# Attention beside a long convolution: QK tiles of 32 rows, zero-weight matmuls in idle row groups, and fillers placed by array use

## The chip, the cores and the metric

The kernel runs on one NeuronCore of one Trainium2 chip. The metric is the device time of one execution in microseconds. The profile is one execution recorded by the hardware profiler; its span is somewhat longer than the timed runs.

## The reference

Two branches work on the same input of 2,048 positions and 448 features and are blended by a gate.

```
q = (x @ wq) in 16 heads of 28;  k = x @ wk;  v = x @ wv     # one k and v for all heads
p = softmax(q k^T / sqrt(28));   a = concat_heads(p v) @ wo
K[d,l] = Re sum_n C[d,n] * exp(dt[d]*A[d,n]*l) * dt[d]*B[d,n]   # N = 256, l = 0..2047
b = causal_convolution(u, K) + u * Dskip                        # written with FFTs of length 4096
out = g * a + (1 - g) * b;       g = sigmoid(sum(x * gate_w))
```

## The kernel before

**Attention.** The scores are made transposed: keys on the 128 output partitions, 512 queries along the free dimension. There are 1,024 such tiles (16 groups of four heads and 512 queries, times 16 key blocks, times 4 heads). A tile is one QK matmul (L1126) whose contraction has 29 rows: 28 features and one row that carries a bound subtracted from the scores. Head h of a group lies on partitions 32h onwards, so that the four heads use the four row groups of the array, each as a tile of 32 rows by 128 columns. `main` packs the tiles into 410 sets, of three heads and two heads in turn; a set fills three or two banks of psS, which has six, so that one set can be made while ScalarE turns the other into exponentials (L1142, one instruction a set). When four tiles of one key block are there, a PV set (L1151) runs: four matmuls of 128 rows by 32 columns, side by side in the column groups, adding into the bank psB. After 16 key blocks psB holds a finished group, ScalarE copies it out, and it is normalised and projected (L1022).

**Convolution.** VectorE builds tables of complex powers (`masters`, `tables`), TensorE turns them into kernel values (`kgen`, L938: 128x32 tiles, 64 columns streamed), these pass through DRAM and come back as Toeplitz tiles T, and `conv` (L985: 128x32 tiles, 128 columns streamed) applies them; L1005 (128x64 tiles) transposes the result, and VectorE adds it to the output.

**Order.** `Prog.op` records each operation with a planned duration `ns`, a mode (`q`: 32x128, `c`: 128x32, `h`: 128x64, `f`: 128x128) and, on TensorE, a number `st` for what it contributes to array activity. `schedule` is a list scheduler that lays all engines out in advance; a change of mode costs 105 ns in the plan (`SWITCH`). Each engine then runs its list strictly in order, with semaphores between engines.

**Fillers.** After scheduling, `fill` walks TensorE's order. Where the plan leaves a gap, it looks at up to eight windows of 3,413 ns, sums `st` in them, and if the sum is under `SCORE` it inserts n filler matmuls with zero weights (each unit planned as `FILL` ns and worth `UNIT`). They write zeros into psB while a PV accumulation is open there (`opened`, start=False), or into an unused bank early on. A filler takes the mode of its neighbours: `q` (L626: one matmul of 32 rows by 128 columns), `f` (L629: one of 128x128) or `c` (L633: four of 128x32). A unit streams 128 columns in all three.

Of the kernel before, what the change touches and what calls it, by code (L numbers as in the profile page):

```python
# [11 lines left out]
P = 128  # L12
# [4 lines left out]
DH = 28  # L17
# [16 lines left out]
RING = 15  # L34
# [45 lines left out]
class Prog:  # L80
# [17 lines left out]
    def op(self, eng, fn, ns, rd=(), wr=(), pr=0, lat=None, lock=None, unlock=None, comm=None, mode="f", st=None, slk=None):  # L98
        o = Op()
        o.i, o.eng, o.fn, o.ns, o.lat, o.pr = len(self.ops), eng, fn, ns, 0, pr  # L100
        o.lock, o.unlock, o.slot, o.ndma = lock, unlock, None, 0
        o.comm = comm
        o.mode, o.slk = mode, slk
        o.st = st or (0.0075 * ns if eng == "pe" else 0.0)
        o.lat = self.LAT[eng] if lat is None else lat
        deps = {}
        if comm is not None:
            for k in comm:
                deps[self.lastw[k]] = 1
                self.commops.setdefault(k, []).append(o.i)  # L110
        for k in rd:
            for c in self.commops.get(k, ()):
                deps[c] = 1
            w = self.lastw.get(k)
            if w is not None:
                deps[w] = 1
        for k in wr:
            w = self.lastw.get(k)
            if w is not None:
                deps[w] = 1  # L120
            for r in self.readers.get(k, ()):
                deps.setdefault(r, 0)
        for k in rd:
            self.readers.setdefault(k, []).append(o.i)
        for k in wr:
            self.lastw[k] = o.i
            self.readers[k] = []
        deps.pop(o.i, None)
        o.deps = deps
        self.ops.append(o)  # L130
        return o
# [222 lines left out]


class Kernel:
    FILL = 90.0
    WIN = 3413.0
    UNIT = 0.56
    SCORE = 17.0  # L360
    nfill = 0

    def __init__(self, nc, ins, out):
# [250 lines left out]
    def fill(self):  # L614
        pg = self.pg
        order, out = pg.order["pe"], []
        used = min(i for i, x in enumerate(order) if pg.ops[x].lock is not None and pg.ops[x].lock.bank == 5)
        opened, prev = False, None

        def filler(n, mode, bank, acc):  # L620
            t, bo = self.bank(bank)

            def fn(e):
                for _ in range(n):
                    if mode == "q":
                        r = e.matmul(t.v(0, P, bo, [[1, 128]]), self.zero.v(0, 32, 0, [[1, P]]), self.ident.v(0, 32, 0, [[1, P]]),  # L626
                                     start=not acc, stop=False, tile_position=(0, 0), skip_group_check=True)
                    elif mode == "f":
                        r = e.matmul(t.v(0, P, bo, [[1, 128]]), self.zero.v(0, P, 0, [[1, P]]), self.ident.v(0, P, 0, [[1, P]]),  # L629
                                     start=not acc, stop=False, tile_position=(0, 0), skip_group_check=True)  # L630
                    else:
                        for j in range(4):
                            r = e.matmul(t.v(32 * j, 32, bo, [[1, 128]]), self.zero.v(0, P, 0, [[1, 32]]), self.ident.v(0, P, 0, [[1, P]]),  # L633
                                         start=not acc, stop=False, tile_position=(0, 32 * j), skip_group_check=True)
                return r
            o = Op()
            o.i, o.eng, o.fn, o.ns, o.lat, o.pr, o.mode = len(pg.ops), "pe", fn, 0, 0, 0, mode
            o.lock = o.unlock = o.slot = o.comm = None
            o.ndma, o.extra, o.end = 0, 0, 0.0
            o.deps = {self.zop.i: 1, self.iop.i: 1}  # L640
            pg.ops.append(o)
            return o.i
        act = [(o.end - o.lat - o.ns, o.st) for o in (pg.ops[x] for x in order)]
        for k, x in enumerate(order):
            o = pg.ops[x]
            start = o.end - o.lat - o.ns
            if prev is None:
                e0, m0 = max(self.zop.end, self.iop.end) + 60.0, "f"
            else:
                e0, m0 = prev.end - prev.lat, prev.mode  # L650
            room = start - e0 - (pg.SWITCH if m0 != o.mode else 0.0) - 60.0
            need = 0.0
            if room > self.FILL and (opened or k < used):
                for w0 in range(8):
                    a = e0 - self.WIN * w0 / 8.0
                    got = sum(d for u, d in act if a <= u < a + self.WIN)
                    need = max(need, self.SCORE - got)
            n = int(min(room, need * self.FILL / self.UNIT) / self.FILL)
            if n > 0:
                mode = m0 if m0 in ("c", "f") else o.mode if o.mode in ("c", "f", "q") else "q"  # L660
                out.append(filler(n, mode, 6 if opened else 5, opened))
                act.append((e0, self.UNIT * n))
                self.nfill += n
            out.append(x)
            pv = self.pvs.get(x)
            if pv is not None:
                opened = pv < 15
            prev = o
        pg.order["pe"], self.wact = out, act
# [250 lines left out]
    def kgen(self, c, sub=None):  # L920
        pg = self.pg
# [5 lines left out]
        whole = sub is None  # L927
# [3 lines left out]
        for jj in range(8):  # L931
            def mm(e, comp, jj=jj):
                for half in range(2):
                    for g in gs:
                        o = 64 * (g // 2) + 16 * half + 8 * (g % 2) + jj
                        fo = lo + comp * BLK + EW + o
                        mo = FM + comp * 64 + o - 32 * (g // 2)
                        r = e.matmul(  # L938
                            G.v(32 * g, 32, 64 * jj, [[1, 64]]),
                            tab.v(0, P, lo + comp * BLK + 32 + o, [[EW, 32]]),  # L940
                            tab.v(0, P, fo, [[mo - fo, 2], [EW, 32]]),
                            start=(comp == 0 and half == 0), stop=(comp == 1 and half == 1),
                            tile_position=(0, 32 * g), skip_group_check=True)
                return r
            for comp in range(2):
                pg.op("pe", lambda e, mm=mm, comp=comp: mm(e, comp), 226 if whole else 113, mode="c", st=1.41 if whole else 0.7,
                      rd=keys, wr=[X] + k1 + k2, pr=1.7, lock=G if jj == 0 and comp == 0 else None)
        pg.op("dve", lambda e: e.tensor_tensor(self.kstg.v(p0, np, 63, [[64, 8]]), G.v(p0, np, 63, [[64, 8]]),
                                               self.skt.v(p0, np, 8 * c, [[1, 8]]), ALU.add),
# [7 lines left out]
        for g in gs:  # L957
            for h in range(2):
# [3 lines left out]
               pr=0, eng="pool", extra=2000)  # L962
# [9 lines left out]
    def conv(self, c):  # L972
        pg = self.pg
        X = ("cx", c)
        co, ck = 512 * (c % NCST), ("cst", c % NCST)
# [3 lines left out]
        for k in range(4):  # L979
            gi = 4 * c + k  # L980
            s = gi % NTR
            for n in range(8):
                def mm(e, k=k, n=n, s=s, gi=gi):
                    for j in range(4):
# [3 lines left out]
                                     start=(n == 0), stop=(n == 7), tile_position=(0, 32 * j), skip_group_check=True)  # L988
                    return r
                first = k == 0 and n == 0  # L990
                pg.op("pe", mm, (94, 92, 90, 82, 76, 70, 58, 57)[n], st=0.72 - 0.03 * n, mode="c", rd=[("T", s)] + [("U", q) for q in range(3)],
                      wr=[X] + ([ck] if first else []), pr=1.8,
                      lock=ps if first else None)
        pg.op("dve", lambda e: e.tensor_tensor(self.cst.v(0, P, co, [[128, 4], [64, 2], [1, 64]]),
# [3 lines left out]
        Y = ("yx", c)  # L998
# [9 lines left out]
                                 start=(mu == 0), stop=(mu == 1), tile_position=(0, 64 * par), skip_group_check=True)  # L1008
            return r
        for k in range(4):  # L1010
            pg.op("pe", lambda e, k=k: yt(e, k), 75, st=0.7, mode="h", rd=[ck, "id"], wr=[Y], pr=1.3)
        ov = self.O.v(0, P, 15 * D + 16 * c, [[-D, 16], [1, 16]])
        pg.op("dve", lambda e: e.tensor_tensor(ov, ov, ps.v(0, P, 0, [[1, 16], [16, 16]]), ALU.add),
              el(256), rd=[Y], slk=SLK[2], comm=tuple(("O", q) for q in range(4)), pr=2, unlock=ps)
# [92 lines left out]
    def main(self):  # L1107
        pg = self.pg
        kT, qT, expT, vaug = self.kT, self.qT, self.expT, self.vaug
        NTL = 1024  # L1110
        self.pvs = {}
        sets, t = [], 0
        while t < NTL:
            n = min(2 if len(sets) % 2 else 3, NTL - t)
# [4 lines left out]
        def qk(s):  # L1119
# [3 lines left out]
            def mm(e):  # L1123
                for k, t in enumerate(ts):
                    i, kt, h = dec(t)
                    r = e.matmul(self.psS.v(0, P, 512 * (bo + k), [[1, 512]]),  # L1126
                                 kT.v(32 * h, DH + 1, 128 * kt, [[1, 128]]),
                                 qT.v(32 * h, DH + 1, 512 * (i % 2), [[1, 512]]),
                                 start=True, stop=True, tile_position=(32 * h, 0), skip_group_check=True)
                return r  # L1130
            rd = set()
            for t in ts:
                i, kt, h = dec(t)
                rd |= {("q", i % 2), ("kT", kt // 4)}
            bk = [("b", bo + k) for k in range(len(ts))]
            pg.op("pe", mm, 220, st=0.61 * len(ts), rd=sorted(rd, key=str), wr=bk, pr=0, mode="q")
            n = 512 * len(ts)
            es = ts[0] % RING
            ew = [("e", t % RING) for t in ts]
# [5 lines left out]
        def pv(v):  # L1145
            ts = range(4 * v, 4 * v + 4)

            def mm(e):
# [3 lines left out]
                                 expT.v(0, P, 512 * (t % RING), [[1, 512]]),  # L1152
                                 start=(kt == 0), stop=(kt == 15), tile_position=(0, 32 * h), skip_group_check=True)
                return r
            o = pg.op("pe", mm, 230, rd=["va"] + [("e", t % RING) for t in ts], wr=[("b", 6)], pr=0.5, mode="c", st=2.1)
            i, kt, h = dec(4 * v)
            self.pvs[o.i] = kt
            if kt == 15 and i < 15:
# [78 lines left out]
```

## Time and profile before

Three timed runs: 558.37, 559.13 and 561.53 us; the median is 559.13. The profile spans 566.2 us.

| Work (line, engine) | Count | Mean of one, ns | Busy, us |
|---|---|---|---|
| exp, 3 heads, 128x1536 (L1142, ScalarE) | 205 | 1,526 | 312.9 |
| exp, 2 heads, 128x1024 (L1142, ScalarE) | 204 | 1,102 | 224.8 |
| QK, 29 rows x 128 columns, 512 streamed (L1126) | 1,024 | 437 | 184.6 |
| PV, 128x32, 512 streamed (L1151) | 1,024 | 441 | 115.8 |
| kernel values into psS and psX (L938) | 1,792 | 294, 292 | 77.5 |
| filler `c`, 128x32, 128 streamed (L633) | 1,176 | 260 | 40.1 |
| filler `q`, 32x128, 128 streamed (L626) | 249 | 271 | 27.4 |

A matmul's mean includes its passage through the array, and matmuls overlap, so the times of a row do not add up to engine time; the distance between two starts tells more. Exps overlap a little as well. A line of stages gives, for a stretch of the span, its length, the busy time of each engine with the number of instructions, the clock that was granted to TensorE as a share of full speed, and what the DMA engines did.

### The profile page before, as it was taken

How to read it: one execution, taken by the hardware profiler on the slowest of the kernel's cores; microseconds unless marked ns; L12 is line 12 of the kernel's file. 1: busy time of each engine (PE TensorE's matmuls, PEld its weight loads, DVE VectorE, ACT ScalarE, POOL GpSimd, SP SyncE). 2: the span in 40 equal slices, each digit the busy share in tenths (PEclk: the TensorE clock that was granted, in tenths of full speed). 3: DMA queues.
4: the chain of work that ended last, by engine and by line, in shares of the span. 5: the costliest groups of instructions: out<-in, count | busy, mean ns of one | idle time of the engine just before them, and what ended most of it. 6: DMA issues, size and time to landing. Idle time of an engine off the chain costs nothing.

```text
span 566.2 us, 21348 instructions
## 1 busy us (share of the span) xinstructions
PE 511.2 (90%) x9725; PEld 282.7 (50%) x9741; DVE 450.2 (80%) x885; ACT 500.8 (88%) x457; POOL 139.8 (25%) x282
## 2 busy tenths in 40 slices
PE   6799999999899899998999989898989897998884
PEld 5445455555555445554555545454545454454552
DVE  8959698997999889999999989999999983212113
ACT  4778899989999889999999989999999995689980
POOL 2000110514114313315050614141334133302100
PEclk9755557559999969999999969999999885589897
DMA  8921010395796986789977988977878856589933
GB/s 237 260 111 39 12 48 2 103 387 190 285 340 234 326 293 255 252 331 298 417 279 278 362 281 279 357 271 278 338 266 347 331 205 254 202 303 387 417 110 130
DMA packets 37666, 142.90 MB, mean 252 GB/s; under 512 B 9920, under 2 KB 20712, under 8 KB 23240
## 3 DMA queue, kind: packets, MB, share of 16 engines
q1 hardware_dynamic: 27656, 135.29, 64.7%
q0 software_dynamic: 8384, 6.09, 4.4%
q8 instruction: 76, 1.25, 0.9%
q10 hardware_dynamic: 1536, 0.17, 0.3%
q14 instruction: 14, 0.11, 0.1%
HBM read 135.38 MB, written 5.74 MB: 249 GB/s over the span
## 4 chain that ended last, share of the span: by engine, by line
PE 40%; ACT 36%; DVE 20%; issue 2%; DMA 2%; ACTq 0%; another core or an unknown queue 0%
ACT expT L1142 35%; PE psS L1126 12%; PE psB L1151 8%; PE psS L938 4%; DVE tab L893 3%; PE psX L938 3%; PE psB L633 3%; PE psB L626 2%; DVE tab L912 2%; PE psX L985 2%; DVE tab L899 2%; DMA sz<-in_A_wv_dram 2%; DVE tmp L895 2%; DVE tab L900 2%; PE psS L985 2%
## 5 line engine op out<-in xcount | busy, mean ns | idle before, releaser
L1142 ACT ACTIVATE expT<-psS 128x1536 bf16<-128x1536 f32 (+1 forms) x410 | 474.7, 1313 | 35.7 <-PE psS L1126 31.5
L1126 PE MATMUL psS<-qT,kT 29*128 29x512 bf16 x1024 | 184.6, 437 | 26.3 <-ACT expT L1142 17.7
L1151 PE MATMUL psB<-expT,vaug 128*32 128x512 bf16 x1024 | 115.8, 441 | 0.8 <-ACT expT L1142 0.4
L1126 PEld LDWEIGHTS psS<-qT,kT 29*128 29x128 bf16 x1024 | 42.2, 93 | 95.1 <-ACT expT L1142 63.4
L137 POOL DMA_DIRECT2D KP_scratch<-kstg x127 | 68.2, 545 | 66.3 <-ACT kstg L951 66.3
L893 DVE TENSOR_TENSOR tab<-tab,mbf 128x256 bf16<-128x256 bf16 (+5 forms) x75 | 69.5, 927 | 1.1
L137 POOL DMA_DIRECT2D denT<-acc x60 | 29.8, 503 | 143.6 <-ACT acc L1040 138.9
L1151 PEld LDWEIGHTS psB<-expT,vaug 128*32 128x32 bf16 x1024 | 27.0, 95 | 73.6 <-issue 71.0
L985 PE MATMUL psX<-T,U 128*32 128x128 bf16 (+7 forms) x2048 | 57.7, 244 | 2.1 <-issue 1.7
L985 PEld LDWEIGHTS psX<-T,U 128*32 128x32 bf16 (+7 forms) x2048 | 50.4, 162 | 13.8 <-issue 10.3
L137 POOL DMA_DIRECT2D rdenB<-R_scratch x60 | 29.8, 503 | 68.2 <-DMA R_scratch<-denT 68.0
L985 PE MATMUL psS<-T,U 128*28 128x128 bf16 (+7 forms) x1536 | 44.3, 247 | 0.5 <-DVE O L1031 0.2
L938 PE MATMUL psS<-tab 128*32 128x64 bf16 x1024 | 42.7, 294 | 2.1 <-issue 2.1
L985 PEld LDWEIGHTS psS<-T,U 128*28 128x28 bf16 (+7 forms) x1536 | 38.2, 160 | 9.6 <-issue 7.4
L633 PE MATMUL psB<-ident,zero 128*32 128x128 bf16 x1176 | 40.1, 260 | 0.9 <-issue 0.9
L895 DVE TENSOR_TENSOR tmp<-tab,mbf 128x256 bf16<-128x256 bf16 (+4 forms) x62 | 39.6, 639 | 0.0
L938 PE MATMUL psX<-tab 128*32 128x64 bf16 x768 | 34.8, 292 | 4.0 <-DVE tmp L907 3.5
L137 POOL DMA_DIRECT2D R_scratch<-denT x15 | 8.6, 576 | 118.8 <-DVE denT L1046 86.5
L938 PEld LDWEIGHTS psS<-tab 128*32 128x32 bf16 x1024 | 30.7, 139 | 12.0 <-issue 9.6
L633 PEld LDWEIGHTS psB<-ident,zero 128*32 128x32 bf16 x1176 | 29.0, 115 | 14.4 <-issue 11.4
L912 DVE TENSOR_TENSOR tab<-tab,tmp 128x2048 bf16<-128x2048 bf16 x28 | 33.7, 1220 | 0.2
L938 PEld LDWEIGHTS psX<-tab 128*32 128x32 bf16 x768 | 26.3, 138 | 10.8 <-issue 5.3
(146 smaller groups left out, 582.5 us busy)
## 6 DMA issues: line engine op xcount, KB each, us to landing
T<-KP_scratch SPq DMA_DIRECT2D x112, 1072.0 KB, 9.1
rdenB<-R_scratch POOLq DMA_DIRECT2D x60, 64.0 KB, 5.5
U<-in_A_x_dram SPq DMA_DIRECT2D x3, 896.0 KB, 14.6
tab<-in_A_x_dram SPq DMA_DIRECT2D x4, 448.0 KB, 7.3
KP_scratch<-kstg POOLq DMA_DIRECT2D x112, 16.0 KB, 4.7
SZ_scratch<-tab SPq DMA_DIRECT2D x1, 1344.0 KB, 5.2
out_dram<-O SPq DMA_DIRECT2D x3, 448.0 KB, 3.8
sz<-SZ_scratch SPq DMA_DIRECT2D x3, 384.0 KB, 4.1
```

Of the source, the lines that this page charges most:

```text
L137: return [e.dma_start(o, i, **kw) for o, i in pairs]
L626: r = e.matmul(t.v(0, P, bo, [[1, 128]]), self.zero.v(0, 32, 0, [[1, P]]), self.ident.v(0, 32, 0, [[1, P]]), start=not acc, stop=False, ti ...
L633: r = e.matmul(t.v(32 * j, 32, bo, [[1, 128]]), self.zero.v(0, P, 0, [[1, 32]]), self.ident.v(0, P, 0, [[1, P]]), start=not acc, stop=Fals ...
L893: vo(lambda e, dst=dst, src=src, mr=mr: e.tensor_tensor(dst, src, mr, ALU.mult), 2 * n, done + mk(lv), kr + ki)
L895: vo(lambda e, src=src, mi=mi, w=w, n=n, tb=tb, to=to: e.tensor_tensor(tb.v(0, P, to, [[n, 2], [cw, w], [1, cw]]), src, mi, ALU.mult), 2 * ...
L899: vo(lambda e, do=do, n=n, to=to, one=one, oth=oth: e.tensor_tensor(one(do), one(do), oth(to + n), ALU.subtract), n, tk + kr, kr)
L912: vo(lambda e, h=h: e.tensor_tensor(tab.v(0, P, FM + 32 * h, [[64, 2], [EW, 32], [1, 32]]), tab.v(0, P, lo + 31 * EW + 64 * h, [[BLK, 2], ...
L938: r = e.matmul(G.v(32 * g, 32, 64 * jj, [[1, 64]]), tab.v(0, P, lo + comp * BLK + 32 + o, [[EW, 32]]), tab.v(0, P, fo, [[mo - fo, 2], [EW, ...
L985: r = e.matmul(ps.v(32 * j, 32 - 2 * n, 128 * k, [[1, 128]]), self.U.v(0, P, 2 * n * D + 4 * gi + j, [[D, 32 - 2 * n]]), self.T.v(0, P, s ...
L1126: r = e.matmul(self.psS.v(0, P, 512 * (bo + k), [[1, 512]]), kT.v(32 * h, DH + 1, 128 * kt, [[1, 128]]), qT.v(32 * h, DH + 1, 512 * (i % 2 ...
L1142: pg.op("act", lambda e: e.activation(expT.v(0, P, 512 * es, [[1, n]]), self.psS.v(0, P, 512 * bo, [[1, n]]), AF.Exp, scale=SQ), 50 + n / ...
L1151: r = e.matmul(self.psB.v(32 * h, 32, 0, [[1, 512]]), vaug.v(0, P, 32 * kt, [[1, 32]]), expT.v(0, P, 512 * (t % RING), [[1, 512]]), start= ...
```

## The change

It concerns only TensorE's instructions and the plan of fillers.

- QK contracts over 32 rows in place of 29. Rows 29 to 31 hold zeros in both operands.
- A two-head QK set leaves two of the four row groups idle. While a PV accumulation is open in psB, two matmuls with zero weights now follow the two QK matmuls in the same operation, one in each idle row group: 32 rows by 64 columns, 512 columns streamed, one into partitions 0 to 63 of psB and one into 64 to 127. The operation's semaphore is set by its last matmul.
- The `q` filler is gone. A filler is now `c` where one neighbour is `c`, else `f` where one is `f`, else `c`; between two neighbours that share another mode, two changes of mode are taken off the room, and at least three units must fit.
- The numbers `st` are set anew in proportion to rows x columns x streamed columns, with an addition for short matmuls; `SCORE` is 33 after the first convolution and 40 (`EARLY`) before it, `FILL` 75 ns.

The purpose is to bring the share of the array in use[...] up where the kernel has idle rows or planned gaps.

```diff
-        o.st = st or (0.0075 * ns if eng == "pe" else 0.0)
+        o.st = st or (0.0175 * ns if eng == "pe" else 0.0)
...
-    FILL = 90.0
+    FILL = 75.0
     WIN = 3413.0
-    UNIT = 0.56
-    SCORE = 17.0
+    UNIT = 1.54
+    SCORE = 33.0
+    EARLY = 40.0
+    conv0 = 10 ** 9
...
-                    if mode == "q":
-                        r = e.matmul(t.v(0, P, bo, [[1, 128]]), self.zero.v(0, 32, 0, [[1, P]]), self.ident.v(0, 32, 0, [[1, P]]),
-                                     start=not acc, stop=False, tile_position=(0, 0), skip_group_check=True)
-                    elif mode == "f":
+                    if mode == "f":
...
+        opn = False
+        for x in order:
+            if x in self.pvs:
+                opn = self.pvs[x] < 15
+            elif x in self.qks and opn:
+                self.qks[x].append(True)
+                pg.ops[x].st += 1.27
...
-                    need = max(need, self.SCORE - got)
+                    need = max(need, (self.SCORE if late else self.EARLY) - got)
+            mode = "c" if "c" in (m0, o.mode) else "f" if "f" in (m0, o.mode) else "c"
+            if m0 == o.mode and mode != m0:
+                room -= 2 * pg.SWITCH
             n = int(min(room, need * self.FILL / self.UNIT) / self.FILL)
-            if n > 0:
-                mode = m0 if m0 in ("c", "f") else o.mode if o.mode in ("c", "f", "q") else "q"
+            if n > (0 if mode in (m0, o.mode) else 2):
...
-                                 kT.v(32 * h, DH + 1, 128 * kt, [[1, 128]]),
-                                 qT.v(32 * h, DH + 1, 512 * (i % 2), [[1, 512]]),
+                                 kT.v(32 * h, 32, 128 * kt, [[1, 128]]),
+                                 qT.v(32 * h, 32, 512 * (i % 2), [[1, 512]]),
                                  start=True, stop=True, tile_position=(32 * h, 0), skip_group_check=True)
+                if open_[-1] is True:
+                    for k, h in enumerate(sorted(set(range(4)) - {t % 4 for t in ts})):
+                        r = e.matmul(self.psB.v(64 * k, 64, 0, [[1, 512]]), self.zero.v(32 * h, 32, 0, [[1, 64]]),
+                                     self.ident.v(32 * h, 32, 0, [[0, 4], [1, P]]),
+                                     start=False, stop=False, tile_position=(32 * h, 64 * k), skip_group_check=True)
                 return r
...
-            pg.op("pe", mm, 220, st=0.61 * len(ts), rd=sorted(rd, key=str), wr=bk, pr=0, mode="q")
+            o = pg.op("pe", mm, 220, st=1.135 * len(ts), rd=sorted(rd, key=str) + ["zero", "id"], wr=bk, pr=0, mode="q")
```

The `st` of PV goes from 2.1 to 4.54, of `kgen` from 1.41 to 2.08, of `conv` from 0.72 - 0.03 n to 1.54 - 0.0625 n, of L1005 from 0.7 to 1.5.

More of the change, by code (lines that the diff above doesn't have):

```diff
@@ L642, in filler @@
             return o.i
+        opn = False
[5 more added lines that the diff above has]
+                pg.ops[x].st += 1.27
         act = [(o.end - o.lat - o.ns, o.st) for o in (pg.ops[x] for x in order)]
+        late = False
         for k, x in enumerate(order):
             o = pg.ops[x]
+            late = late or x == self.conv0
             start = o.end - o.lat - o.ns
@@ L945, in kgen @@
             for comp in range(2):
-                pg.op("pe", lambda e, mm=mm, comp=comp: mm(e, comp), 226 if whole else 113, mode="c", st=1.41 if whole else 0.7,
+                pg.op("pe", lambda e, mm=mm, comp=comp: mm(e, comp), 226 if whole else 113, mode="c", st=2.08 if whole else 1.04,
                       rd=keys, wr=[X] + k1 + k2, pr=1.7, lock=G if jj == 0 and comp == 0 else None)
@@ L990, in conv @@
                 first = k == 0 and n == 0
-                pg.op("pe", mm, (94, 92, 90, 82, 76, 70, 58, 57)[n], st=0.72 - 0.03 * n, mode="c", rd=[("T", s)] + [("U", q) for q in range(3)],
+                self.conv0 = min(self.conv0, len(pg.ops))
+                pg.op("pe", mm, (94, 92, 90, 82, 76, 70, 58, 57)[n], st=1.54 - 0.0625 * n, mode="c", rd=[("T", s)] + [("U", q) for q in range(3)],
                       wr=[X] + ([ck] if first else []), pr=1.8,
@@ L1010, in conv @@
         for k in range(4):
-            pg.op("pe", lambda e, k=k: yt(e, k), 75, st=0.7, mode="h", rd=[ck, "id"], wr=[Y], pr=1.3)
+            pg.op("pe", lambda e, k=k: yt(e, k), 75, st=1.5, mode="h", rd=[ck, "id"], wr=[Y], pr=1.3)
         ov = self.O.v(0, P, 15 * D + 16 * c, [[-D, 16], [1, 16]])
@@ L1110, in main @@
         NTL = 1024
-        self.pvs = {}
+        self.pvs, self.qks = {}, {}
         sets, t = [], 0
@@ L1126, in mm @@
                     r = e.matmul(self.psS.v(0, P, 512 * (bo + k), [[1, 512]]),
-                                 kT.v(32 * h, DH + 1, 128 * kt, [[1, 128]]),
-                                 qT.v(32 * h, DH + 1, 512 * (i % 2), [[1, 512]]),
+                                 kT.v(32 * h, 32, 128 * kt, [[1, 128]]),
+                                 qT.v(32 * h, 32, 512 * (i % 2), [[1, 512]]),
                                  start=True, stop=True, tile_position=(32 * h, 0), skip_group_check=True)
+                if open_[-1] is True:
[3 more added lines that the diff above has]
+                                     start=False, stop=False, tile_position=(32 * h, 64 * k), skip_group_check=True)
                 return r
+            open_ = [ts]
             rd = set()
@@ L1135, in qk @@
             bk = [("b", bo + k) for k in range(len(ts))]
-            pg.op("pe", mm, 220, st=0.61 * len(ts), rd=sorted(rd, key=str), wr=bk, pr=0, mode="q")
+            o = pg.op("pe", mm, 220, st=1.135 * len(ts), rd=sorted(rd, key=str) + ["zero", "id"], wr=bk, pr=0, mode="q")
+            if len(ts) == 2:
+                self.qks[o.i] = open_
             n = 512 * len(ts)
@@ L1154, in mm @@
                 return r
-            o = pg.op("pe", mm, 230, rd=["va"] + [("e", t % RING) for t in ts], wr=[("b", 6)], pr=0.5, mode="c", st=2.1)
+            o = pg.op("pe", mm, 230, rd=["va"] + [("e", t % RING) for t in ts], wr=[("b", 6)], pr=0.5, mode="c", st=4.54)
             i, kt, h = dec(4 * v)
```

## The prediction

> **What bounds the kernel now.** I read the page's busy shares and its 40 slices first, then groups by form, then stages cut where the granted clock changes, then waits and the timeline of TensorE.
>
> ```profile
> PE 511.2 (90%) x9725; PEld 282.7 (50%) x9741; DVE 450.2 (80%) x885; ACT 500.8 (88%) x457; POOL 139.8 (25%) x282
> ACT  4778899989999889999999989999999995689980
> PEclk9755557559999969999999969999999885589897
> ```
>
> ScalarE's row falls from 9 to 8 or less where PEclk is 5 to 7: slices 3 to 9, 14 and 15, 24, 33 to 36. The same in stages (us; PE, PEld, DVE, ACT, POOL busy with instruction counts; clock; DMA share; GB/s), the second block counting only L1142, the exp:
>
> ```profile
> 42.50:90.80 48.30, 47.80 (x596) 24.00 (x600) 42.66 (x111) 43.05 (x38) 4.68 (x9) 0.50 0.09 29
> 101.05:124.90 23.85, 23.85 (x373) 12.87 (x374) 23.78 (x51) 21.72 (x20) 7.99 (x16) 0.50 0.72 249
> 206.90:329.70 122.80, 114.00 (x2553) 65.49 (x2555) 120.28 (x234) 122.10 (x113) 37.60 (x72) 1.00 0.83 306
> 469.70:500.40 30.70, 30.04 (x413) 15.64 (x418) 5.69 (x11) 20.25 (x19) 9.35 (x18) 0.50 0.57 196
> ```
>
> ```profile
> 42.50:90.80 48.30, 42.56 (x37) 0.50 0.09 29
> 206.90:329.70 122.80, 119.26 (x105) 1.00 0.83 306
> 469.70:500.40 30.70, 18.70 (x16) 0.50 0.57 196
> ```
>
> At clock 1.00 the exps bound everything: one per 122.80/105 = 1.170 us, ScalarE busy 99%. At 0.50 TensorE has no idle time and the exps come every 48.30/37 = 1.305 us, late even every 30.70/16 = 1.919 us. So half clock is the loss to be had back: 37 x 0.135 = 5.0 us before 90.8, 19 exps in 23.85 us give 1.6 us before 125, and 16 x 0.749 = 12.0 us at 470 to 500. Three short drops (196.6, 329.7, 449.2) leave ScalarE idle 2.6, 2.8 and 1.2 us. Together about 25 us.
>
> **What the skill says.** "TensorE: Matmul & The Clock Gate", Part 1: the clock stands at half or full, decided in windows of about 3.4 us by how busy the array was. The trace agrees as to the two states (0.50 and 1.00). It does not take the row PE busy for the measure: that row is full at 0.50. So I count array use myself: rows x columns x N of each matmul over 128 x 128, against 8,192 columns that a window of 3.41 us holds at full clock. A 29-row QK head is 116, a PV matmul 128, an L633 matmul 32, an L626 matmul 32, a kernel-generation matmul (L938) 16. The window 97.64 to 101.05, at 1.00, holds 8 QK, 4 PV, 16 L938 and one L798 (448): about 2,150, or 0.26, and the next is at 0.50. The window 121.53 to 124.94, at 0.50, holds 5 QK, 4 PV, 28 L633 and 34 convolution matmuls of about 29: about 3,000, or 0.36, and the next is at 1.00. Attention windows near 105 to 118 with 0.33 to 0.36 stay low. So full clock needs somewhat more than a third of the array, and losing it takes about 0.3.
>
> "TensorEngine Tiling (Array Packing)", Key Properties: changing the tiling mode, not just the tile, drains the engine; its list has 32x128 and 32x64 as different modes. "TensorE: Matmul & The Clock Gate", Part 3: matmuls in different row groups run together, started about 4 ns apart. The trace shows both (start, length):
>
> ```profile
> 236.60 0.39 PE L1126 MATMUL psS<-qT,kT 29*128 29x512 bf16 x2
> 236.92 0.40 PE L1151 MATMUL psB<-expT,vaug 128*32 128x512 bf16 x4
> 237.25 0.45 PE L1005 MATMUL psS<-ident,cst 128*64 128x64 bf16 x16
> ...
> 43.25 0.61 PE L1126 MATMUL psS<-qT,kT 29*128 29x512 bf16 x3
> 43.26 0.28 PE L626 MATMUL psB<-ident,zero 32*128 32x128 bf16 x1
> ```
>
> From 512 columns (0.213 us) to the next mode takes 0.32 to 0.33 us, so a change costs about 0.105 us, also from 128x32 to 128x64, where only the column width changes. But at 43.26 an old filler in an idle row group starts beside QK, at no cost; it has QK's own 32x128 mode. No row shows a 32x64 tile beside a 32x128 one. That is the unknown of this case.
>
> **The change, part by part.** The order of the other instructions on every engine is the planner's as before, since the weights `st` enter only the filler placement.
>
> 1. QK rows 29 to 32: 128 instead of 116 per head, same columns streamed: no time. The three rows are zero on both sides.
> 2. Fillers, counted in the built orders. Until the first convolution matmul (66 QK sets, 42 PV sets): 116 groups of four 128x32 matmuls and 152 L626 become 286 groups and none. A group does four times the array work of an L626 in the same 128 columns. After it: 178 groups, 97 L626 and 23 full ones become 184 groups and 6 full: 108 units fewer, 108 x 0.057 = 6 us less work in TensorE's planned gaps, worth nothing where ScalarE bounds.
>    Array use per pair of sets (5 heads), early: before (165 x 116 + 42 x 512 + 116 x 128 + 152 x 32)/33 = 1,830; after, with part 3, (165 x 128 + 42 x 512 + 286 x 128 + 32 x 128)/33 = 2,525. That is 1.38 times as much. Price: an L626 behind QK needed no change of mode; a group does, some 0.21 us per place and two-set pair, on an engine that is full at half clock (48.30/18.5 = 2.6 us a pair, so 2.8). Array use at half clock then rises by 1.38 x 2.6/2.8 = 1.28: from 0.33-0.36 to 0.42-0.46, above what the 124.9 step needed. At full clock a pair has 2.34 us and TensorE's work in it, two QK (0.63), 1.27 PV (0.27), 8.7 groups (0.50) and three further changes (0.32), is 1.7: hidden behind the exps, and array use is 2,525/(2.34 x 2,400) = 0.45, so the clock holds.
> 3. Zero-weight matmuls: 190 of the two-head sets get two of 32x64x512. They are the last of their op, so the semaphore for the exp comes with them. Behind them on TensorE stand PV, fillers and convolution, and for those the normalisation, VectorE and the loads. Their two weight loads lie in PEld's idle half; the new dependence on the zero and identity tiles is met long before. Low bound: they run beside QK, some 10 ns. High bound: drain and stream, 0.105 + 0.213 = 0.318 us at full clock, 0.105 + 0.427 = 0.53 at half. They add 128 per pair, most useful in the mid, where drops began at 0.29 to 0.35.
>
> I take the low bound: they occupy rows that QK leaves idle, as the L626 at 43.26 did. Then: early 5.0 + 1.6, of which I count 5, since 26 to 45 us stays low (the gap there, 1.76 us before L590, is untouched); short drops 6.6, of which a third, 2, since two begin behind gaps of 1.69 and 1.59 us in TensorE's issue that stay; the late 12.0, of which a third, 4, since it begins behind a 3.5 us wait for VectorE's table (L907) that stays. 559 - 11 = 548.
>
> **Rivals.** *The zero matmuls run after QK, not beside it* (slower). For: the 0.105 us between 128x32 and 128x64, and the skill's list of modes; also the tiling page's Gotcha 1 says that row tiles cannot write one PSUM bank at once, and both write psB (no row of before has that case). Against: no part of the array is wanted twice. TensorE's slack at full clock:
>
> ```profile
> PEld psS L1126 <- ACT expT L1142: 17.8, 51, 0.8
> ...
> PE psS L1126 <- ACT expT L1142: 4.9, 15, 0.6
> ```
>
> These are the waits (us in total, times, longest) between 206.9 and 329.7. The weight loader idles already while the last matmul streams, and TensorE's row counts a matmul past its streaming, so they bound the slack from both sides: 4.9 to 17.8 us over some 52 pairs, 0.09 to 0.34 us a pair. 0.318 us against a middle of 0.21, unevenly spread, loses 0.1 to 0.2 us: at 0.15, 158 sets after the first convolution lose 24 us. Early 32 x 0.53 = 17 us if the clock stays low, little if it rises. Less 5 to 10 for drops avoided: 575 to 595, I say 580.
>
> *They run beside it, but the clock does not rise*: about 32 more changes of mode early cost 3 us, drops avoided give 3 or 4: 558.
>
> **How the numbers follow.** 548 with 0.52, 580 with 0.36, 558 with 0.12. The first spreads from 541 (all early, half the rest) to 555. Range 541 to 583: it leaves out the upper half of the slow case. Faster 0.50 + 0.04, same 0.07, slower 0.36 + 0.03.
>
> **What would show it.** Beside: the 64-column matmuls start within 0.02 us of QK's in the timeline, and the next mode 0.32 us after QK. After: they start 0.32 us behind, the next change as far again, exps at 1.00 come slower than 1.17 us. Clock: slices 4 to 9 of PEclk go to 9. Wrong if that row stays at 5, or if VectorE, 98% busy at 207 to 330, turns out to set the pace.

## The result and the profile after

The changed kernel takes 586.76 us (median; 583.83 to 589.27) against 558.75 for the kernel before in the same comparison. The ratio is 1.049, with an interval of 1.043 to 1.056: slower. The profiled run spans 586.2 us, where the one before spans 566.2. The clock that TensorE is granted varies from one run to the next, for every kernel here, and the time varies with it: the kernel before took 550.9 us at a granted share of 0.912 and 567.0 at 0.867. So a median moves by a per cent or so between comparisons, and each experiment below is read against the runs of the kernel before made beside it. Medians are over all runs; ratios compare only the runs within 1.5% of the fastest of their kernel, so they can differ a little from the quotient of the medians.

The page of the changed kernel, with the three rows that were shown of before (its exp is L1161, QK L1137, the zero-weight matmuls L1143, PV L1170, the `c` fillers L632, the convolution L995):

```profile
PE 549.7 (94%) x10553; PEld 286.8 (49%) x10553; DVE 451.9 (77%) x885; ACT 507.6 (87%) x457; POOL 140.1 (24%) x282
ACT  4768999989887699999899999999999977799960
PEclk9858999999978599999999999999999868799968
```

The clock did rise: slices 5 to 9 are at 9 where they were at 5 to 7, the short drops at 330 and 449 us are gone, and the mean over the span went from 0.858 to 0.920. Not everywhere: two drops, at 158 to 169 and 186 to 203 us, stand where there was one, at 197 to 207. And still ScalarE idles more at full clock: from 220 to 460 us it is busy for 229.64 of 240.00 us (line below), where it was for 122.10 of 122.80. TensorE's busy share went from 90% to 94%. The chain that ended last says the same; it was 40% TensorE and 36% ScalarE before:

```profile
PE 68%; ACT 24%; DVE 3%; issue 2%; DMA 2%; ACTq 0%
```

The stages, first with all engines, then with the exps alone (columns as before):

```profile
42.50:90.80 48.30, 47.49 (x1097) 23.51 (x1089) 44.53 (x114) 45.29 (x41) 4.68 (x9) 0.93 0.10 31
220.00:460.00 240.00, 233.96 (x4744) 124.47 (x4741) 222.88 (x421) 229.64 (x206) 73.52 (x140) 1.00 0.80 291
```

```profile
220.00:460.00 240.00, 223.28 (x191) 1.00 0.80 291
```

Between 220 and 460 us the clock is at 1.00 throughout and an exp comes every 240.00/191 = 1.257 us; before, at the same clock, it was 1.170 in the stage from 206.9 to 329.7. Taken from the starts of the exps in the two traces, the 91st starts at 148.0 us before and 144.7 after, the 391st at 526.6 and 543.3. So the changed kernel is 3.3 us ahead when the convolution is under way, and loses 20.0 us over the next 300 sets. The loss lies at full clock: between these two exps, half clock took 58.0 us before and 54.6 after, and in the rest an exp came every 1.199 us before and every 1.265 after.

What takes the time stands in the timeline of TensorE (start, length):

```profile
238.43 0.39 PE L1137 MATMUL psS<-qT,kT 32*128 32x512 bf16 x2
238.74 0.40 PE L1143 MATMUL psB<-ident,zero 32*64 32x512 bf16 x2
239.07 0.63 PE L995 MATMUL psS<-T,U 128*30 128x128 bf16 x21
```

The zero-weight pair does not start with QK but 0.315 us behind it (median of the starts at full clock). To stream 512 columns takes 0.427 us at half clock, by the distance between two L808 matmuls in a row, so 0.213 at full; that leaves 0.102 for the change of mode. The next work starts 0.328 us after the pair: its streaming and 0.115. In the kernel before, the next mode started 0.315 us behind QK, so each two-head set with a pair now has two changes of mode and two streams where it had one of each. At 0.328 us, 190 sets are 62 us of TensorE.

The slack that was to carry it, in the waits (total, times, longest) between 220 and 460 us:

```profile
PEld psS L1137 <- ACT expT L1161: 14.1, 36, 1.2
...
PE psS L1137 <- ACT expT L1161: 4.2, 10, 0.9
```

Over some 95 pairs of sets that is 0.04 to 0.15 us for two sets, where it was 0.09 to 0.34. TensorE seldom waits for an exp now; the exps wait for TensorE.

### The profile page after: what moved, and what is told of

Read it like the earlier page. It is cut to its first block, busy times and chain, and to the rows that moved or that the text cites. A ratio compares the mean times of both kernels' runs of the same rounds, so it can differ in the third digit from the quotient of the medians.

```text
span 586.2 us, 22988 instructions
## 1 busy us (share of the span) xinstructions
PE 549.7 (94%) x10553; PEld 286.8 (49%) x10553; DVE 451.9 (77%) x885; ACT 507.6 (87%) x457; POOL 140.1 (24%) x282
## 4 chain that ended last, share of the span: by engine, by line
PE 68%; ACT 24%; DVE 3%; issue 2%; DMA 2%; ACTq 0%
ACT expT L1161 23%; PE psS L1137 18%; PE psB L1170 11%; PE psB L1143 8%; PE psX L995 6%; PE psS L948 5%; PE psS L995 5%; PE psX L948 4%; PE psB L632 2%; DMA sz<-in_A_wv_dram 2%; PE psS L808 1%; ACT acc L1051 1%; PE psS L1033 1%; PE psX L808 1%; PE psX L1016 1%
## 5 line engine op out<-in xcount | busy, mean ns | idle before, releaser
L1161 ACT ACTIVATE expT<-psS 128x1536 bf16<-128x1536 f32 (+1 forms) x410 | 479.7, 1256 | 46.5 <-PE psS L1137 34.4
L1137 PE MATMUL psS<-qT,kT 32*128 32x512 bf16 x1024 | 170.6, 410 | 10.4 <-ACT expT L1161 7.6
L1170 PE MATMUL psB<-expT,vaug 128*32 128x512 bf16 x1024 | 108.3, 414 | 0.1
L1143 PE MATMUL psB<-ident,zero 32*64 32x512 bf16 x380 | 80.5, 421 | 0.0
L1137 PEld LDWEIGHTS psS<-qT,kT 32*128 32x128 bf16 x1024 | 39.7, 92 | 77.4 <-ACT expT L1161 32.2
L995 PE MATMUL psX<-T,U 128*24 128x128 bf16 (+7 forms) x2048 | 57.2, 243 | 0.8 <-issue 0.8
L1170 PEld LDWEIGHTS psB<-expT,vaug 128*32 128x32 bf16 x1024 | 26.5, 94 | 63.7 <-issue 63.1
L995 PEld LDWEIGHTS psX<-T,U 128*24 128x24 bf16 (+7 forms) x2048 | 50.1, 162 | 12.6 <-issue 9.8
L632 PE MATMUL psB<-ident,zero 128*32 128x128 bf16 x1880 | 48.0, 228 | 1.7 <-issue 1.7
L995 PE MATMUL psS<-T,U 128*22 128x128 bf16 (+7 forms) x1536 | 44.7, 247 | 3.0 <-issue 3.0
L995 PEld LDWEIGHTS psS<-T,U 128*28 128x28 bf16 (+7 forms) x1536 | 38.3, 161 | 11.9 <-issue 9.8
L1143 PEld LDWEIGHTS psB<-ident,zero 32*64 32x64 bf16 x380 | 20.2, 103 | 47.7 <-issue 47.7
L632 PEld LDWEIGHTS psB<-ident,zero 128*32 128x32 bf16 x1880 | 35.0, 100 | 16.6 <-issue 11.3
```

The costliest lines, as they stand in the source:

```text
L995: r = e.matmul(ps.v(32 * j, 32 - 2 * n, 128 * k, [[1, 128]]), self.U.v(0, P, 2 * n * D + 4 * gi + j, [[D, 32 - 2 * n]]), self.T.v(0, P, s ...
L1137: r = e.matmul(self.psS.v(0, P, 512 * (bo + k), [[1, 512]]), kT.v(32 * h, 32, 128 * kt, [[1, 128]]), qT.v(32 * h, 32, 512 * (i % 2), [[1, ...
L1143: r = e.matmul(self.psB.v(64 * k, 64, 0, [[1, 512]]), self.zero.v(32 * h, 32, 0, [[1, 64]]), self.ident.v(32 * h, 32, 0, [[0, 4], [1, P]]) ...
L1161: pg.op("act", lambda e: e.activation(expT.v(0, P, 512 * es, [[1, n]]), self.psS.v(0, P, 512 * bo, [[1, n]]), AF.Exp, scale=SQ), 50 + n / ...
L1170: r = e.matmul(self.psB.v(32 * h, 32, 0, [[1, 512]]), vaug.v(0, P, 32 * kt, [[1, 32]]), expT.v(0, P, 512 * (t % RING), [[1, 512]]), start= ...
```

## The experiments

The theory: the 32x64 tiles are another mode than QK's 32x128, so the array drains, that is, runs empty, before and after them, and their streaming does not lie beside QK. Its rivals: the new filler places, with their changes of mode and more instructions, cost the time; or it is the two row groups that write one PSUM bank; or any further work in the set, or the semaphore that comes later for the exp.

**No zero-weight matmuls.** All else stands in its place.

```diff
-                if open_[-1] is True:
-                    for k, h in enumerate(sorted(set(range(4)) - {t % 4 for t in ts})):
-                        r = e.matmul(self.psB.v(64 * k, 64, 0, [[1, 512]]), ...
```

> The changed kernel without its 380 zero-weight matmuls, all other instructions in the same places. Theory (each pair of 64-column matmuls drains the array and streams after QK: 0.33 us of TensorE per two-head set, 190 sets, 62 us, most of it not covered by slack): the QK-to-next distance falls from 0.65 to 0.32 us, the rate of exps at full clock returns to about 1.17 us, the early part stays at full clock through the new fillers: 540 to 552 us. Rival (the new filler places with their extra changes of mode, or the larger number of instructions, cost the time): it stays above 570 us.

548.31 us (541.48 to 557.19) beside 560.48 for the kernel before, ratio 0.986 (0.967 to 1.0045). That it is faster than the kernel before is not sure, but it is far from the changed kernel's 583.83 to 589.27. The distance from QK to the next mode is back at 0.315 us. The 91st exp starts at 140.9 us and the 391st at 514.8 in its trace, of the longest of its four runs: 373.9 us for the 300 sets, against 398.6 with the pairs, at nearly the same granted clock (0.935 and 0.931 over that stretch). So the pairs cost 24.7 us there, 0.176 us for each of the 140 pairs in it; the rest of their 0.328 us lay in TensorE's slack. The fillers and their places are not the loss.

**One zero-weight matmul of QK's own tile size.** It has the same array work as the pair.

```diff
-                    for k, h in enumerate(sorted(set(range(4)) - {t % 4 for t in ts})):
-                        r = e.matmul(self.psB.v(64 * k, 64, 0, [[1, 512]]), self.zero.v(32 * h, 32, 0, [[1, 64]]),
-                                     ... tile_position=(32 * h, 64 * k), ...)
+                    h = min(set(range(4)) - {t % 4 for t in ts})
+                    r = e.matmul(self.psB.v(0, P, 0, [[1, 512]]), self.zero.v(32 * h, 32, 0, [[1, P]]),
+                                 ... tile_position=(32 * h, 0), ...)
```

> The changed kernel with one zero-weight matmul of 32 rows by 128 columns (QK's own tile size) in one idle row group in place of two of 32x64; same array work, same place, same semaphore. Theory (the cost is the change of tile size): it starts within 0.01 us of the QK matmuls and costs nothing: within 1% of the kernel without zero-weight matmuls, 540 to 555 us. Rival (any further matmul in the set, a second writer of psB, or the later semaphore costs the time): near the changed kernel, 575 to 590 us.

553.51 us beside 560.48, ratio 0.989 (0.984 to 0.994). Its timeline:

```profile
237.93 0.39 PE L1137 MATMUL psS<-qT,kT 32*128 32x512 bf16 x2
237.93 0.39 PE L1143 MATMUL psB<-ident,zero 32*128 32x512 bf16 x1
238.25 1.19 PE L948 MATMUL psS<-tab 128*32 128x64 bf16 x32
```

The 128-column matmul starts with QK (3 ns behind, median), and the next mode 0.32 us after QK as without it. So an idle row group takes work without delaying the next, in the mode that is running. A further matmul in the set and a write into psB beside QK hold nothing up where they stand. Whether the whole is free is less sure: runs at a granted share of 0.959 and 0.964 took 548.67 and 547.17 us, where one without any zero-weight matmul took 541.48 at 0.961. Such single runs show no more than a hint, and it was not followed.

The later semaphore is not tested by this, since the last matmul is only 3 ns behind QK here. No run tells its share of the loss from that of TensorE's own time; the trace of the changed kernel puts 4.8 us of the exps' waits in the 300 sets, 12 of them, down to L1143, beside the loss of 24.7.

**A single 32x64 matmul.** Half of the pair, which takes the second row group and the shared PSUM bank away.

```diff
-                        r = e.matmul(self.psB.v(64 * k, 64, 0, [[1, 512]]), ... tile_position=(32 * h, 64 * k), ...)
+                    r = e.matmul(self.psB.v(0, 64, 0, [[1, 512]]), ... tile_position=(32 * h, 0), ...)
```

> The changed kernel with a single zero-weight matmul of 32x64 per two-head set in place of two (half the array work in it). Theory (the change from 32x128 to 32x64 drains the array, however many matmuls follow): it starts 0.31 to 0.32 us behind QK, like the pair, and the time stays near the changed kernel, 580 to 595 us. Rival (the pair is slow because two row groups write one PSUM bank): it starts beside QK and the time falls to about that of the kernel with one 32x128 matmul, 545 to 557 us.

604.13 us (586.89 to 620.71) beside 563.04: above what was expected. The runs spread too widely for a ratio, and their times follow their clocks (0.91 for the fastest, 0.845 for the slowest); but even the fastest is where the changed kernel is. And its timeline decides:

```profile
236.06 0.39 PE L1137 MATMUL psS<-qT,kT 32*128 32x512 bf16 x2
236.38 0.40 PE L1143 MATMUL psB<-ident,zero 32*64 32x512 bf16 x1
236.71 0.34 PE L995 MATMUL psS<-T,U 128*20 128x128 bf16 x8
```

It starts 0.32 us behind QK like the pair, and the next work 0.328 us behind it, as behind two. In the changed kernel the two matmuls of a pair start 3 to 4 ns apart in every one of 190 sets, so sharing the bank's halves held neither up. The rival of the PSUM bank is out.

**Short zero-weight matmuls**, 128 columns instead of 512.

```diff
-                        r = e.matmul(self.psB.v(64 * k, 64, 0, [[1, 512]]), ...
+                        r = e.matmul(self.psB.v(64 * k, 64, 0, [[1, 128]]), ...
```

> The changed kernel with the 32x64 zero-weight matmuls streaming 128 columns instead of 512. Theory (change of mode 0.10 us plus streaming): a set costs 0.10 + 0.053 = 0.17 us instead of 0.33, so 190 x 0.16 = 30 us of TensorE less; the time falls to 555 to 572 us, between the kernel without them and the changed kernel. Rival (only the drain counts, streaming lies beside other work): 580 to 590 us, as with 512 columns.

577.47 us (559.28 to 592.04) beside 560.48: the median is outside what was expected. The cost in place is near what the theory says:

```profile
235.76 0.39 PE L1137 MATMUL psS<-qT,kT 32*128 32x512 bf16 x2
236.08 0.24 PE L1143 MATMUL psB<-ident,zero 32*64 32x128 bf16 x2
236.25 0.97 PE L995 MATMUL psS<-T,U 128*30 128x128 bf16 x40
```

0.168 us from the pair to the next work in place of 0.328; the sum that was expected, 0.10 + 0.053, is 0.15, and the change back takes 0.115. The four times follow the granted clocks: 559.28 us, inside what was expected, at 0.959, then 574.26, 580.69 and 592.04 at 0.901, 0.899 and 0.864. The trace is of the last:

```profile
PEclk9999998879795995999557999999998558569997
```

A stretch of it at full clock can still be read, exps alone, and beside it one of the kernel without zero-weight matmuls:

```profile
317.60:454.20 136.60, 129.79 (x114) 1.00 0.83 304
326.30:459.50 133.20, 129.23 (x113) 1.00 0.84 309
```

An exp comes every 1.198 us, and every 1.179 without; with the long pairs it was 1.257. So at full clock the short pairs lose much less, as the theory says. Drains stay and array work goes, which would lower the array's use; that this is why three of the four runs got a lower clock than the changed kernel's 0.909 to 0.927 is argued, not shown.

**The kernel before with the pairs alone** (29-row QK and the old fillers stay).

```diff
+                if open_[-1] is True:
+                    for k, h in enumerate(sorted(set(range(4)) - {t % 4 for t in ts})):
+                        r = e.matmul(self.psB.v(64 * k, 64, 0, [[1, 512]]), self.zero.v(32 * h, 32, 0, [[1, 64]]), ...
```

> The kernel before with only the two 32x64 zero-weight matmuls added to its two-head sets (29-row QK and old fillers stay). Theory: 190 x 0.33 us at full clock, 0.53 at half, less the slack: 580 to 605 us, more than the changed kernel if its fillers win the early clock. Rival (the added array work raises the clock enough to pay for them): 555 to 570 us.

618.10 us beside 560.48, ratio 1.114 (1.106 to 1.123): further than expected. The trace is of its longest run, 631.03 us. The clock and one set at half clock:

```profile
PEclk9995555555989955999995599999999967799697
```

```profile
237.10 0.61 PE L1132 MATMUL psS<-qT,kT 29*128 29x512 bf16 x2
237.64 0.63 PE L1138 MATMUL psB<-ident,zero 32*64 32x512 bf16 x2
238.20 1.22 PE L991 MATMUL psS<-T,U 128*32 128x128 bf16 x36
```

At half clock the pair comes 0.54 us behind QK and holds the next work back by 0.56, on an engine that was full already (48.05 of the 48.30 us from 42.5 to 90.8). Without the new fillers the early part stays at half clock: the 91st exp starts at 170.1 us, 22 later than before. In the changed kernel the fillers paid for this part, and what was left was the middle.

**29 rows, new fillers, no zero-weight matmuls.** This tells the 32 rows from the fillers.

```diff
-                                 kT.v(32 * h, 32, 128 * kt, [[1, 128]]),
-                                 qT.v(32 * h, 32, 512 * (i % 2), [[1, 512]]),
+                                 kT.v(32 * h, DH + 1, 128 * kt, [[1, 128]]),
+                                 qT.v(32 * h, DH + 1, 512 * (i % 2), [[1, 512]]),
```

> The changed kernel without zero-weight matmuls and with QK over 29 rows again: the new fillers alone. Theory (the gain of the early part comes from the fillers; 32 rows add only 12 columns of array work a head, about 96 per window of 3.4 us against 8,192): within 1.5% of the kernel without zero-weight matmuls, 542 to 557 us, with full clock early. Rival (32 rows are what lifts the clock): 556 to 565 us, early clock at half.

553.15 us beside 563.04, ratio 0.978 (0.968 to 0.989). Its early stage:

```profile
42.50:90.80 48.30, 41.67 (x1059) 21.22 (x1061) 47.61 (x123) 48.30 (x45) 8.68 (x17) 1.00 0.12 31
```

Full clock, ScalarE busy throughout, 45 instructions on it against 38 before. The fillers alone bring the gain; the three more rows show no effect that these runs could tell.

**More fillers after the first convolution**, with the 32x128 matmul.

```diff
-    SCORE = 33.0
+    SCORE = 40.0
```

> The changed kernel with one 32x128 zero-weight matmul per two-head set, and the score of 40 for the whole kernel (687 filler units instead of 529). Theory (array use keeps the clock, and fillers in planned gaps cost little at full clock): fewer drops after 125 us, 538 to 552 us, faster than before. Rival (TensorE is too full after the first convolution for more fillers): 555 to 565 us.

566.72 us beside 563.04, ratio 1.0105 (1.003 to 1.018). The theory expected a gain; the time is a little above even the rival's range. The trace is of its longest run (580.37 us). The stage from 220 to 460 us in three parts, exps alone:

```profile
220.00:300.00 80.00, 69.90 (x60) 0.91 0.72 268
300.00:380.00 80.00, 72.70 (x63) 0.94 0.85 304
380.00:460.00 80.00, 74.63 (x66) 0.96 0.80 294
```

Counted by their starts, since the lines count an exp at a border twice, that is 187 exps, where the same kernel with the score of 33 has 194, at a clock of 0.96 over that stretch. But the clock is not all of it. Of its timed runs, three at 0.951 to 0.955 still took over 561 us. And at full clock, this kernel and then the one with the score of 33:

```profile
347.00:449.40 102.40, 96.95 (x84) 1.00 0.81 298
323.80:439.90 116.10, 113.19 (x100) 1.00 0.83 303
```

An exp comes every 1.219 us with the added fillers and every 1.161 without. Which instructions they held up was not followed further.

**Fewer fillers after the first convolution**, with the 32x128 matmul and with none.

```diff
-    SCORE = 33.0
+    SCORE = 25.0
```

> The changed kernel with one 32x128 zero-weight matmul per two-head set and the score after the first convolution lowered from 33 to 25 (373 filler units instead of 529; the early 40 stays). Theory (after the first convolution TensorE is nearly full, fillers there cost as much as the clock they keep; the early fillers are the gain): 543 to 556 us, a little faster than before, like the same kernel with 33. Rival (the later fillers are needed for the clock): more drops, 556 to 570 us.

> The changed kernel without zero-weight matmuls (and without their share in the placement) and with the score of 25 after the first convolution (393 filler units). Theory as for the other: 543 to 556 us. Rival (the free 32x128 matmul is what keeps the clock when fillers are few): slower than its sister by 5 us or more.

551.00 and 551.42 us beside 564.40, ratios 0.982 (0.975 to 0.989) and 0.980 (0.971 to 0.989): both beat the kernel before and the changed one, and they do not differ. Fewer late fillers do not lose the clock enough to show in the time. The 32x128 matmul brings nothing that shows in it either, though the granted clock was 0.907 to 0.947 with it and 0.891 to 0.918 without.

A kernel whose exp is released by QK itself, with the pair behind it, was not tried. It would tell the later semaphore from the time on TensorE.

## Why the prediction was wrong

*The step that failed* is in part 3: "I take the low bound: they occupy rows that QK leaves idle, as the L626 at 43.26 did." That filler has QK's mode and the pair has not. The runs show 0.315 us from QK to the pair and 0.328 from it to the next work, where it was 0.315 without a pair: 0.328 us more for a set, the high bound of the prediction (0.318) and not the low one (some 10 ns). A single 32x64 matmul shows the same; a 32x128 one starts 3 ns behind QK. Of that, 0.176 us a pair reached the exps. The 0.105 us between 128x32 and 128x64 in the profile before, where the row count stays and only the column width changes, was the nearer row, and the Trainium skill's "TensorEngine Tiling (Array Packing)", Key Properties, says that a change of mode, not of tile alone, drains the engine; the 0.102 and 0.115 us here agree. Both were quoted and put with the rival. The argument against them, that no part of the array is wanted twice, does not count: the pair's rows were idle, and it waited all the same.

*The clock* was right in the early part. The new fillers raise it: slices 5 to 9 at 9, and 42.5 to 90.8 us at 0.93 against 0.50. In the middle it was right only in part: between the 91st and the 391st exp, half clock went from 58.0 us to 54.6. And the measure behind it is weaker than it was put. Counted in the prediction's way over the 3.41 us windows of the trace before, those at half clock that a rise followed hold 0.24 to 0.44 of the array, and others without a rise up to 0.37. No line between them comes out, so that 0.42 to 0.46 would be enough was a guess that came true. Nor did all three short drops begin at 0.29 to 0.35: the window before the one at 329.7 us holds about 0.2. In the first reading, too, ScalarE's row is not at 8 or less throughout slices 3 to 9: slices 6 to 8 are at 9.

*The sum.* Without the pairs the kernel takes 548.31 us, where 548 was forecast for pairs that cost nothing. That it agrees so closely is luck: the four runs spread from 541 to 557, and the forecast counted on the pairs' array work. Against the trace before, the one without pairs is 7.1 us ahead at the 91st exp, where 5 were counted, and gains 4.6 more up to the 391st; 6 were counted for the drops.

*The slow rival* (580) had the mechanism and was a little low. It took 0.15 us lost per set after the first convolution, 24 us: 0.176 was measured, over 140 pairs and 24.7 us, against the kernel without pairs. It counted 5 to 10 us back for drops avoided; the whole way from 548.31 to 586.76 us is 38, of the 62 that the pairs take on TensorE. How much of that was waiting for the later semaphore is open.

*The third case*, no rise of the clock, did not come.

*PSUM*: the Trainium skill's "TensorEngine Tiling (Array Packing)", Gotcha 1, says that row tiles cannot use a PSUM bank at once. For two that write different halves of its partitions the runs show otherwise: they start 3 to 4 ns apart, and the next work comes 0.328 us behind two as behind one.

## What to carry to other kernels

In these runs idle rows of the array took work without delay only in the tile size that was running. Look in the timeline for the distance between the last matmul of one size and the first of the other before filling them. A cost that the profile does not show is better taken from the nearest row that changes the same thing (here the column width) than from the row that looks like it in purpose. And where two engines are both about full, raising the clock of one with more work on it is worth only what its slack can carry: 32x128 zeros delayed nothing where they stood and won nothing, the new fillers won some 2%, most of it in the early part of the trace, and more fillers later lost it.

## What was not expected of the hardware

The change from 32x128 to 32x64 takes 0.102 us at full clock and 0.107 at half, though the matmuls lie in different row groups, and the change back to a 128-row mode 0.115 and 0.133. So it hardly grows at half clock, while 512 columns go from 0.213 us to 0.427. Shortening the pair's streaming by three quarters saved 0.16 us a set in place, but the four runs took 559 to 592 us as their granted clock went from 0.959 down to 0.864.
